# A fused BigBird attention and FNet mixer on one core: another order and split of the last output stores, and in the second batch a mask that moves between TensorE and VectorE by the planner's reckoning

## The chip, the cores and the metric

The kernel runs on one core of one Trainium2 chip. The metric is the device time of one execution in microseconds. The kernel before was timed six times: median 1064.39 us, from 1063.14 to 1068.95. "PE" is TensorE, "DVE" VectorE, "ACT" ScalarE, "POOL" GpSimd, and "SP" SyncE, which issues most of the DMAs.

## The reference

Four batches, eight heads, 768 positions, head width 64, all float32. Attention with a block mask (blocks of 32: neighbours, first and last block, three random blocks per row), then a Fourier mix, a normalization and a two-layer channel product:

```python
scores = np.where(mask, scale * q @ k.T, -1e9)
attn   = exp(scores - max); attn /= attn.sum(-1)          # per head
x      = (attn @ v), heads side by side                    # (4, 768, 512)
u      = x + real(fft(fft(x, axis=1), axis=2))
un     = (u - mean(u)) / sqrt(var(u) + 1e-6)
out    = u + relu(un @ w_ch1) @ w_ch2                      # 512 -> 2048 -> 512
```

## The kernel before

**Order.** Everything is written out in one order by hand-made Python loops (a manual schedule); each engine runs its instructions in that order. The order is chosen while the program is built by a planner: `when["PE"]`, `when["ACT"]`, `when["DVE"]` and `when["POOL"]` are its reckoned clocks, `busy` advances one, `bank` and `give` stand for PSUM banks. What it reckons is a guess with fixed prices; what it puts out is an order.

**Attention.** Two heads make a pair, four pairs a batch (`pairs`, numbered n from 0 to 15). A pair has two halves of 384 queries, and each half has six units, one for each 128 keys, so there are 192 units, numbered u0 to u191; u48 to u95 are the second batch. A slot is two units. For a unit, `scores` (L569) puts the products of two heads into one of two PSUM tiles `s`; `weigh` turns them into weights `e` (one of four SBUF tiles); `values` (L642) multiplies them by v one slot later, and `gather` adds them up over the keys into `acc` for the softmax sums.

The mask is applied in one of two ways. For a unit in `by_pe`, PE adds a product of two small bf16 factors to the scores (L579), and ACT takes the exponent straight into `e` (L589). For the others ACT takes the exponent in place in PSUM (L597), and DVE multiplies by the 0/1 mask and writes `e` (L599). In the first case the `s` tile is free after ACT, in the second after DVE. The line that decides is

```python
if n < NP or masks["by_pe"]:
    by_pe.add(u)
```

where n < NP is the first batch, and `masks["by_pe"]` becomes False in `go`, the step that puts the first batch's channel products into the queue `late`. In this kernel that happens just before u100. `gather` lets DVE add (L623, both heads in one instruction) where the unit is in `by_pe` and the planner's clocks say that DVE is sooner; otherwise POOL adds (L628, one instruction per head).

**The mixer** of batch b runs beside the attention of batch b+1. Its steps before the channel products stand in `apart` and are put in by `gap` wherever the planner sees room: `norm_steps`, the folds (L774 to L802), `along` and `across` (Fourier products), `spread` and `whiten` (normalization, with two small POOL instructions for the root at L913 and L915), `un_flip` (four transposes, tile `utp`, L965, copied by ACT at L966), and `right` (differences for the channel products, L1002). The channel products are fast-multiplication schemes with seven products instead of eight: `quad` (L1040) for the first layer, `channels` (L1096) for the second, and for the last batch `outputs` (L1159).

**x and its stores.** `place` turns a pair's output (transposes `xt`, L665) and ACT copies it into `x` (L666). There are two x tiles for each half of the positions, so batch b reuses the tile of batch b-2 and ACT has to wait until the stores of that tile have landed. `store` (L1107) writes one third (m) of a half; `_rows` gives the row patterns. For half 0, m = 0 and 2, it is two DMAs of 64 rows; for half 1, m = 0 and 2, it is one DMA of 2x64 rows; m = 1 is 1 + 63 + 63 + 1 rows in half 0 and 1 + 2x63 + 1 in half 1. SP issues them in order.

**The last outputs.** `outputs(r, m, after)` runs for r = 0, 1 and m = 0, 1, 2, and r = 1 stores. Each call makes seven products p (PSUM tiles `m` with two buffers, `t` and `o` with one, `s` with two), and DVE adds them into a0, a1 (columns 0:256 and 256:512 of half 0) and b0, b1 (of half 1). `ahead(1)` to `ahead(4)` are the DVE differences that the next m needs. In the kernel before the seven products end in a0, a0, u, b1 and a1, u, a1, b0, and for the last m the stores stand so: b1 after the fifth product, half 0 whole after the sixth, and b0 at the very end, in two pieces of 128 columns, one issued by SP and one by ACT.

After the stores every engine meets `tc.If(over > 0)` (L1574), a branch over a general version that these inputs do not take, and the program ends when all DMAs have landed.

Of the kernel before, what the change touches and what calls it, by code (L numbers as in the profile page):

```python
# [82 lines left out]
def _rows(view, tile):  # L83

    got = []
    for t, p0, runs, jump, n, s0, step in _ORDER:
        if t != tile:
            continue
        at = view[s0:s0 + 1, :]
        row, col = list(at.ap[0])[0], list(at.ap[1])  # L90
        if jump > 0:
            got.append((p0, runs * n, bass.AP(tensor=at.tensor, offset=at.offset,
                                              ap=[[jump * row, runs], [step * row, n], col])))
            continue
        for r in range(runs):
            at = view[s0 + r * jump:s0 + r * jump + 1, :]
            got.append((p0 + r * n, n, bass.AP(tensor=at.tensor, offset=at.offset,
                                               ap=[[step * row, n], col])))
    return got
# [3 lines left out]
def kernel(  # L103
# [14 lines left out]
    nc = tc.nc  # L118

    B, H, S, D = q.shape  # L120
    DM = H * D
    FF = w_ch1.shape[1]
    P = 128
# [14 lines left out]
    NP = H // 2  # L138
# [43 lines left out]
    ps_s = ctx.enter_context(tc.tile_pool(name="ps_s", bufs=2, space=PSUM))  # L182
    ps_o = ctx.enter_context(tc.tile_pool(name="ps_o", bufs=1, space=PSUM))
# [5 lines left out]
    when = {"PE": 0.0, "ACT": 0.0, "DVE": 0.0, "POOL": 0.0}  # L189
    free = {"m": [0.0, 0.0], "t": [0.0]}  # L190

    def busy(engine, us, after=0.0):
        when[engine] = max(when[engine], after) + us
        return when[engine]
# [283 lines left out]
    by_pe, to_gather = set(), deque()  # L478
    masks = {"by_pe": True}
# [68 lines left out]
    UP = 2 * C  # L548
    UNITS = len(pairs) * UP
    SLOT = 2  # L550

    def scores(us):

        n, w = divmod(us[0], UP)
        half = w // C
        qT, kT = turned[n, 0], turned[n, 1]
        queries = slice(half * HS, (half + 1) * HS)
        got = []
        for u in us:
            c = u % C  # L560
            s = ps_s.tile([P, 2, 512], FP32, tag="s", name="s")
            got.append((u, s))
            if n < NP or masks["by_pe"]:
                by_pe.add(u)
            busy("PE", 0.72, max(e_at.get(u - SLOT, 0.0), z_at[u % 2]))
            s_at[u] = when["PE"] + HOP
            for i in range(2):
                rows = slice(D * i, D * i + D)
                nc.tensor.matmul(s[:, i, 0:HS], kT[rows, c * P:(c + 1) * P], qT[rows, queries],  # L569
                                 start=True, stop=u not in by_pe)  # L570
        for u, s in got:
            if u not in by_pe:
                continue
            c = u % C
            busy("PE", 0.25)
            s_at[u] = when["PE"] + HOP
            for i in range(2):
                rows = slice(D * i, D * i + D)
                nc.tensor.matmul(s[:, i, 0:HS], of_k[rows, c * P:(c + 1) * P], off_q[rows, queries],  # L579
                                 start=False, stop=True)  # L580
        return got
# [24 lines left out]
    def gather_to(u):  # L606
        while to_gather and to_gather[0] <= u:
            gather(to_gather.popleft())

    def gather(u):  # L610


        n, w = divmod(u, UP)
        half, c = divmod(w, C)
        if c == 0:
            return
        if c == 1:
            acc_of[n, half] = acc_p.tile([P, 2, HS], FP32, tag="acc", name="acc")
        acc, e = acc_of[n, half], e_of[u]
        start = e_of[u - 1] if c == 1 else acc  # L620
        at = max(e_at[u], acc_at.get((n, half), 0.0))
        if u in by_pe and masks["by_pe"] and w < UP - SLOT and max(when["DVE"], at) + 1.0 < max(when["POOL"], at) + 2.9:
            nc.vector.tensor_tensor(out=acc, in0=start, in1=e, op=ALU.add)  # L623
            acc_at[n, half] = busy("DVE", 1.0, at) + HOP
        else:

            for i in range(2):
                nc.gpsimd.tensor_add(out=acc[:, i, :], in0=start[:, i, :], in1=e[:, i, :])  # L628
            acc_at[n, half] = busy("POOL", 2.9, at) + HOP
        e_free[u] = acc_at[n, half]  # L630
# [320 lines left out]
    def mixer(b, xA, xB):  # L951
# [24 lines left out]
        t, s = {}, {}  # L976
# [127 lines left out]
        def store(half, m, cols=slice(0, DM), queue=nc.sync):  # L1104
            x = (xA, xB)[half]
            for p0, cnt, rows in _rows(out[b][:, cols], T * half + m):
                queue.dma_start(out=rows, in_=x[p0:p0 + cnt, m, cols])  # L1107
            if m == T - 1:
                finished.add((b, half))
# [5 lines left out]
        o_t, o_s = {}, {}  # L1115
        DH = DM // 2

        def block(r, k, n):
            return w2_sb[:, 8 * r + 4 * k:8 * r + 4 * k + 4, n * DH:n * DH + DH]
# [25 lines left out]
        def outputs(r, m, after):  # L1145

            if m == 0:
                output_left(m, 1)
                output_left(m, 2)
            a11, a12, a21, a22 = (hs[g, i][:, :, m * P:(m + 1) * P]  # L1150
                                  for i in range(2) for g in range(2))
            a0, a1 = xA[:, m, 0:DH], xA[:, m, DH:DM]
            b0, b1 = xB[:, m, 0:DH], xB[:, m, DH:DM]
            rights = {j: [o_t[j, 0], o_t[j, 1]] for j in (1, 2, 3, 4)}

            def product(pool, tag, a, c):
                ps = pool.tile([P, 512], FP32, tag=tag, name="yy")[:, 0:DH]
                for k in range(4):
                    nc.tensor.matmul(ps, a[:, k, :],  # L1159
                                     c[k // 2][:, k % 2, :] if isinstance(c, list) else c[:, k, :],  # L1160
                                     start=(k == 0), stop=(k == 3))
                busy("PE", 1.75)
                return ps

            def plus(to, a, c=None):
                tt(out=to, in0=a, in1=to if c is None else c, op=ALU.add)
                busy("DVE", 0.43)

            def ahead(j):
                if after is not None:  # L1170
                    output_left(after, j)

            u = sum_p.tile([P, DH], FP32, tag="oT", name="u")
            p1 = product(ps_m, "m", a11, block(r, 0, 0))
            nc.scalar.copy(out=u, in_=p1)
            plus(a0, p1)
            plus(a0, product(ps_m, "m", a12, block(r, 1, 0)))
            if m == 0:
                output_left(m, 3)
                output_left(m, 4)  # L1180
            plus(u, product(ps_t, "t", a21, rights[2]), u)
            plus(a1, u)
            p5 = product(ps_o, "o", o_s[m, 1], rights[1])
            plus(a1, p5)
            ahead(1)
            plus(u, product(ps_s, "s", o_s[m, 3], rights[3]), u)
            both = xB[:, m, :].rearrange("p (n d) -> p n d", n=2)
            tt(out=both, in0=both,
               in1=u.rearrange("p (o d) -> p o d", o=1).broadcast_to([P, 2, DH]), op=ALU.add)
            busy("DVE", 0.7)  # L1190
            plus(b1, p5)
            ends = r == 1 and after is None
            if ends:
                store(1, m, slice(DH, DM))
            ahead(2)
            p3 = product(ps_m, "m", o_s[m, 4], block(r, 1, 1))
            plus(a1, p3)
            if r == 1:
                store(0, m)
            ahead(3)  # L1200
            ahead(4)
            plus(b0, product(ps_s, "s", a22, rights[4]))
            if ends:
                store(1, m, slice(0, P))
                store(1, m, slice(P, DH), nc.scalar)
            elif r == 1:
                store(1, m)

        fl = [[("tm"[h == 1 and m != 1], lambda h=h, m=m: un_flip(h, m), 0.6, 0.55, 0.0)
               for m in range(T)]  # L1210
# [6 lines left out]
              for m, us in (((0, 2), RIGHT), ((1,), COMBINE))]  # L1217
        le = [("d", lambda i=i: left(0, i), 0.0, 0.0, COMBINE) for i in (1, 3, 4)]
        after = ([fl[0][0], sp[1][0]] + le +
                 [fl[0][2], sp[1][2], wh[1][0], fl[0][1], sp[1][1], wh[1][2],  # L1220
                  fl[1][0], fl[1][2], wh[1][1]] + ri[0] + [fl[1][1]] + ri[1])
        rest = []
        for r in range(2 if last else 0):
            rest += [(lambda p=p: quad(p), 7 * PRODUCT) for p in range(4 * r, 4 * r + 4)]
            rest += [(lambda r=r, m=m: outputs(r, m, m + 1 if m + 1 < T else None), 7 * 1.75)
                     for m in range(T)]
# [123 lines left out]
    def slot(sl):  # L1350
# [21 lines left out]
        if paired and len(due) == 2 and due[0] % SP % T == T - 1:  # L1372
            sum_up()
        got = scores(units) if sl < B * SB else ()
        if paired and len(due) == 2:
            sum_up()
# [236 lines left out]
```

## Time and profile before

| | |
|---|---|
| median of six executions | 1064.39 us |
| the profiled execution: its own time / its span | 1066.16 us / 1064.4 us |
| mean granted TensorE clock | 0.994 |
| PE busy | 1037.8 us, 98% of the span |
| L579 mask product on PE, 200 instructions | 327 ns each, 24.9 us together |
| L597 exponent in PSUM, ACT / L589 exponent to `e`, ACT | 792 / 815 ns |
| L599 mask on DVE | 951 ns (92 times) |
| L623 accumulation on DVE / L628 accumulation on POOL | 1039 ns (17 times) / 1043 ns per head |
| L1166 addition of a product, DVE / L1142 difference, DVE | 423 / 684 ns |

The busy share of PE counts overlapping matmuls once. A wait is read from the timeline: the gap before an instruction stands in brackets with what ended it.

The last stores, from the trace (issue: start of the issuing instruction; landing: last completion event). PE's last matmul ends at 1053.15 us. Where a DMA is 64 or 63 rows, 16 or 9 separate completions are seen; where it is 2x64 or 2x63 rows, two.

| issued, us | by | rows x bytes | landed, us |
|---|---|---|---|
| 1028.12 | SP | 64 x 2048 | 1030.42 |
| 1029.65 | SP | 2x64 x 2048 | 1037.60 |
| 1042.01 | SP | 2x63 x 2048 | 1049.98 |
| 1051.36 | SP | 2x64 x 1024 | 1056.26 |
| 1051.99 | SP | 64 x 2048 | 1057.36 |
| 1052.56 | SP | 64 x 2048 | 1058.55 |
| 1053.63 | SP | 2x64 x 512 | 1061.26 |
| 1053.63 | ACT | 2x64 x 512 | 1062.30 |

The packets of the 2x64 stores with 1024-byte rows run from 1052.53 to 1055.92 us; those of 512-byte rows from SP run from 1057.36 to 1060.90 and from ACT from 1059.28 to 1061.75. SP's first wait for completions ends at 1062.32, and the span ends 2.1 us later.

### The profile page before, as it was taken

What the parts mean: (1) busy time and instruction counts of PE and PEld (TensorE: products, weight loads), DVE (VectorE), ACT (ScalarE), POOL (GpSimd) and SP (SyncE); (2) the same over time, 40 slices, a digit from 0 to 9 for tenths busy, and PEclk for the clock granted to TensorE, in tenths of its full rate; (3) what the DMA queues carried; (4) which work ended last, traced back from release to release, by engine and by line L of the source; (5) the groups of instructions that cost most, each with busy time, mean ns of one, the idle gap of its engine ahead of it and who ended that gap; (6) DMA issues with size and microseconds to landing.
All of it is one profiled execution on the core that took longest, in us unless ns stands there. A gap on an engine that the chain in (4) does not pass through costs nothing.

```text
span 1064.4 us, 12409 instructions
## 1 busy us (share of the span) xinstructions
PE 1037.8 (98%) x4390; PEld 537.1 (50%) x4390; DVE 654.5 (61%) x1218; ACT 374.2 (35%) x742; POOL 235.6 (22%) x262
## 2 busy tenths in 40 slices
PE   8989999999999999999999999999999999999995
PEld 4433445444455554444444555444445554578584
DVE  5888995667645445664668364765457355574663
ACT  6978755664030112343441302353221211210210
POOL 1000073537000001454553001256520001000000
PEclk9999999999999999999999999999999999999998
DMA  7756522220000002212230001221000001000001
GB/s 208 223 178 214 133 46 39 52 47 15 1 0 1 1 0 47 59 29 54 42 55 1 1 0 30 60 38 27 11 11 5 1 0 34 27 0 1 1 20 42
DMA packets 120741, 46.65 MB, mean 44 GB/s; under 512 B 108114, under 2 KB 113632, under 8 KB 120672
## 3 DMA queue, kind: packets, MB, share of 16 engines
q1 hardware_dynamic: 118654, 44.92, 17.1%
q10 hardware_dynamic: 1986, 0.85, 0.3%
q8 instruction: 36, 0.59, 0.2%
q14 instruction: 33, 0.27, 0.1%
q0 software_dynamic: 32, 0.01, 0.0%
HBM read 37.11 MB, written 6.29 MB: 41 GB/s over the span
## 4 chain that ended last, share of the span: by engine, by line
PE 90%; DVE 3%; ACT 2%; DMA 2%; issue 1%; POOL 0%; SPq 0%; ACTq 0%; POOLq 0%; DVEq 0%
PE y L1096 23%; PE z L1040 15%; PE s L569 12%; PE o L642 11%; PE yp L1040 7%; PE yy L1159 7%; PE xp L1040 4%; PE zp L850 2%; PE s L579 1%; DMA out_dram<-x 1%; PE sp L709 1%; PE zp L822 1%; PE sp L723 1%; PE utp L965 1%; PE xt L665 1%
## 5 line engine op out<-in xcount | busy, mean ns | idle before, releaser
L628 POOL TENSOR_TENSOR acc<-acc,e 128x384 f32<-128x384 f32 x158 | 159.3, 1043 | 94.1 <-DVE e L599 75.1
L569 PE MATMUL s<-qT,kT 64*128 64x384 f32 x768 | 153.8, 516 | 8.8 <-ACT e L589 5.3
L642 PE MATMUL o<-e,vr 128*64 128x384 f32 x768 | 142.0, 497 | 0.0
L1096 PE MATMUL y<-w_sb,hB 128*128 128x512 f32 x288 | 128.2, 596 | 1.0 <-DVE x L1099 1.0
L1096 PE MATMUL y<-w_sb,hA 128*128 128x512 f32 x288 | 128.4, 595 | 0.0
L599 DVE TENSOR_TENSOR e<-s,mask 128x768 f32<-128x768 f32 x92 | 83.9, 951 | 57.7 <-ACT s L597 48.0
L1099 DVE TENSOR_TENSOR x<-y,x 128x512 f32<-128x512 f32 x72 | 49.7, 691 | 110.9 <-PE y L1096 110.7
L569 PEld LDWEIGHTS s<-qT,kT 64*128 64x128 f32 x768 | 64.0, 186 | 86.9 <-issue 22.1
L597 ACT ACTIVATE s<-s 128x768 f32<-128x768 f32 x92 | 69.9, 792 | 87.6 <-PE s L569 87.0
L628 POOL TENSOR_TENSOR acc<-e 128x384 f32<-128x384 f32 x42 | 47.1, 1142 | 213.9 <-ACT e L589 128.9
L1040 PE MATMUL z<-unT,t 128*128 128x384 f32 x256 | 93.1, 486 | 1.2 <-DVE hA L1045 1.2
L1045 DVE TENSOR_TENSOR hA<-z,hA 128x384 f32<-128x384 f32 x64 | 35.7, 558 | 87.2 <-PE z L1040 87.2
L589 ACT ACTIVATE e<-s 128x768 f32<-128x768 f32 x100 | 76.1, 815 | 36.9 <-PE s L579 31.8
L1096 PEld LDWEIGHTS y<-w_sb,hB 128*128 128x128 f32 x288 | 53.4, 190 | 67.7 <-issue 64.8
L913 POOL TENSOR_SCALAR st<-st 128x1 f32<-128x1 f32 x24 | 8.6, 358 | 346.9 <-DVE st L912 346.9
L1096 PEld LDWEIGHTS y<-w_sb,hA 128*128 128x128 f32 x288 | 53.3, 190 | 62.8 <-issue 59.7
L642 PEld LDWEIGHTS o<-e,vr 128*64 128x64 f32 x768 | 48.0, 136 | 70.5 <-issue 68.1
L1049 ACT ACTIVATE hA<-hA 128x384 f32<-128x384 f32 x64 | 33.5, 523 | 120.3 <-DVE hA L1045 119.9
L1040 PEld LDWEIGHTS z<-unT,t 128*128 128x128 f32 x256 | 48.5, 190 | 35.5 <-DVE hA L1045 2.1
L1049 ACT ACTIVATE hB<-hB 128x384 f32<-128x384 f32 x64 | 33.5, 523 | 86.5 <-DVE hB L1045 84.2
L1060 ACT COPY hA<-xp 128x384 f32<-128x384 f32 x32 | 15.3, 478 | 97.9 <-PE xp L1040 97.9
L1040 PE MATMUL xp<-unT,w_sb 128*128 128x384 f32 x128 | 47.2, 492 | 0.0
(202 smaller groups left out, 1433.2 us busy)
## 6 DMA issues: line engine op xcount, KB each, us to landing
wraw<-in_moe_w_ch_dram SPq DMA_DIRECT2D x32, 512.0 KB
vr<-in_v_dram SPq DMA_DIRECT2D x30, 192.0 KB
qb<-in_q_dram SPq DMA_DIRECT2D x44, 96.0 KB
kb<-in_k_dram SPq DMA_DIRECT2D x44, 96.0 KB
x<-oT SPq DMA_DIRECT2D x192, 12.0 KB
out_dram<-x SPq DMA_DIRECT2D x17, 128.0 KB
out_dram<-x SPq DMA_DIRECT2D x7, 256.0 KB
qr<-in_q_dram SPq DMA_DIRECT2D x24, 64.0 KB
```

The costliest lines, as they stand in the source:

```text
L569: nc.tensor.matmul(s[:, i, 0:HS], kT[rows, c * P:(c + 1) * P], qT[rows, queries], start=True, stop=u not in by_pe)
L589: nc.scalar.activation(out=e, in_=s[:, :, 0:HS], func=ACT.Exp, scale=scale)
L597: nc.scalar.activation(out=s[:, :, 0:HS], in_=s[:, :, 0:HS], func=ACT.Exp, scale=scale)
L599: nc.vector.tensor_tensor(out=e, in0=s[:, :, 0:HS], in1=m.broadcast_to([P, 2, HS]), op=ALU.mult)
L628: nc.gpsimd.tensor_add(out=acc[:, i, :], in0=start[:, i, :], in1=e[:, i, :])
L642: nc.tensor.matmul(o[D * i:D * i + D, :], vt[:, i, c, :], e[:, i, :], start=(c == 0), stop=(c == C - 1))
L1040: nc.tensor.matmul(to, a[:, k, :], c[:, k, :], start=(k == 0), stop=(k == ND // 2 - 1))
L1045: tt(out=to, in0=ps, in1=a, op=ALU.add)
L1049: nc.scalar.activation(out=h, in_=h, func=ACT.Relu)
L1096: nc.tensor.matmul(y, hs[0, half][:, l, m * P:(m + 1) * P], w2_sb[:, 4 * r + l, :], start=(l == 0), stop=(l == 3))
L1099: nc.vector.tensor_tensor(out=x[:, m, :], in0=y, in1=x[:, m, :], op=ALU.add)
L1159: nc.tensor.matmul(ps, a[:, k, :], c[k // 2][:, k % 2, :] if isinstance(c, list) else c[:, k, :], start=(k == 0), stop=(k == 3))
```

## The change

Three places change.

1. In `scores` a unit of the second batch is masked by PE only where the planner's DVE clock is more than 1 us past its PE clock, and otherwise by DVE.
2. In `outputs` the order of the products becomes a0, a0, u, b0, u, b1 and a1, a1; three of the four `ahead` differences move behind the sixth product's additions.
3. The stores move with them. For the last m the half 0 store is split into columns 0:256 (after the second product) and 256:512 (at the very end), and the half 1 store into columns 0:256 (after the fifth product, from ACT) and 256:512 (after the sixth product, from SP). For m = 0 and 1 the half 1 store now comes before the half 0 store.

```diff
+        behind_pe = when["DVE"] > when["PE"] + 1.0
-            if n < NP or masks["by_pe"]:
+            if n < NP or masks["by_pe"] and behind_pe:
                 by_pe.add(u)
...
+            ends = r == 1 and after is None
             plus(a0, product(ps_m, "m", a12, block(r, 1, 0)))
+            if ends:
+                store(0, m, slice(0, DH))
...
             plus(a1, u)
-            p5 = product(ps_o, "o", o_s[m, 1], rights[1])
-            plus(a1, p5)
-            ahead(1)
+            plus(b0, product(ps_s, "s", a22, rights[4]))
             plus(u, product(ps_s, "s", o_s[m, 3], rights[3]), u)
             both = xB[:, m, :].rearrange("p (n d) -> p n d", n=2)
             tt(out=both, in0=both, in1=u..., op=ALU.add)
+            if ends:
+                store(1, m, slice(0, DH), nc.scalar)
+            p5 = product(ps_o, "o", o_s[m, 1], rights[1])
             plus(b1, p5)
-            ends = r == 1 and after is None
-            if ends:
-                store(1, m, slice(DH, DM))
+            if r == 1:
+                store(1, m, slice(DH if ends else 0, DM))
+            plus(a1, p5)
+            ahead(1)
             ahead(2)
+            ahead(3)
             p3 = product(ps_m, "m", o_s[m, 4], block(r, 1, 1))
             plus(a1, p3)
             if r == 1:
-                store(0, m)
-            ahead(3)
+                store(0, m, slice(DH if ends else 0, DM))
             ahead(4)
-            plus(b0, product(ps_s, "s", a22, rights[4]))
-            if ends:
-                store(1, m, slice(0, P))
-                store(1, m, slice(P, DH), nc.scalar)
-            elif r == 1:
-                store(1, m)
```

In `gather` the condition of the accumulation only gets a name (`sooner`).

Because the planner's clocks depend on the choice, the built program changes in more places than the diff. Put side by side, the two instruction orders differ so on PE:

- u50/51, u68/69, u70/71, u88/89 and u96/97 lose the PE mask, u102/103 get it (before, they were masked by DVE); so 92 units instead of 100 have the PE mask, 16 mask matmuls fewer, and 8 DVE masks more.
- The last `un_flip` of the first batch moves from the slot of u96 to just behind u100/101; `go` comes later, and the first `quad` starts behind u106/107 instead of behind u102/103.
- One set of three small transposes (`st`, L736) moves behind the values of u50/51, and another into that first `quad`.
- One third of the first batch's last `channels` step (half 1, m = 0) and an `un_flip` move from behind u110/111 to before the `xt` transposes and u108/109. Its store now stands ahead of a k load on SP's queue.
- From there on PE's order is the same up to `outputs`. On the other queues, two units' accumulations move from DVE to POOL overall (15 instead of 17 on DVE).

## The prediction

> **What bounds the kernel now.** I read the page's busy shares and its chain first, then the order in which the changed program's instructions stand, then the timeline at each place where the two orders differ.
>
> ```profile
> PE 1037.8 (98%) x4390; PEld 537.1 (50%) x4390; DVE 654.5 (61%) x1218; ACT 374.2 (35%) x742; POOL 235.6 (22%) x262
> ...
> PE 90%; DVE 3%; ACT 2%; DMA 2%; issue 1%; POOL 0%; SPq 0%; ACTq 0%; POOLq 0%; DVEq 0%
> ```
>
> PE is the bound. So a change counts by the PE work it takes away, by the PE gaps it makes or closes, and by the 11 us after PE's last matmul. A masked slot of the second batch, in the timeline:
>
> ```profile
> 202.42 1.56 PE L569 MATMUL s<-qT,kT 64*128 64x384 f32 x8
> 203.82 0.49 PE L579 MATMUL s<-factors 64*128 64x384 bf16 x4
> 204.24 1.51 PE L642 MATMUL o<-e,vr 128*64 128x384 f32 x8
> ```
>
> From the last score matmul to the first of `values` it is 0.74 us here and 0.42 in the slot of u100, which has no PE mask: the PE mask costs 0.32 us a slot. Next, the start of the channel products:
>
> ```profile
> 241.97 1.78 PE L569 MATMUL s<-qT,kT 64*128 64x384 f32 x8 [0.41 <-DVE e L599]
> ...
> 246.14 3.88 DVE L751 TENSOR_TENSOR x<-x,r 128x512 f32<-128x512 f32 x3
> ...
> 250.54 0.59 PE L1040 MATMUL z<-unT,t 128*128 128x384 f32 x1 [1.15 <-DVE hA L1045]
> ```
>
> PE waits 0.41 us at u102 (and 0.11 at u103) because DVE masked u100/101 late, and 1.15 us in the first `quad`, because three L751 stood ahead of the sum it needs. Then two places where ACT stands still for the stores of the x tile that it is to refill:
>
> ```profile
> 411.37 1.11 SPq L1107 DMA_DIRECT2D out_dram<-x  x2
> ...
> 414.65 0.48 ACT L666 COPY x<-xt 128x384 f32<-128x384 f32 x1 [2.98 <-DMA kb<-in_k_dram]
> ...
> 416.88 0.92 PE L569 MATMUL s<-qT,kT 64*128 64x384 f32 x4 [1.28 <-DVE e L599]
> ```
>
> ```profile
> 443.04 0.48 ACT L666 COPY x<-xt 128x384 f32<-128x384 f32 x1 [1.85 <-DMA out_dram<-x]
> ...
> 445.32 0.92 PE L569 MATMUL s<-qT,kT 64*128 64x384 f32 x4 [0.74 <-DVE e L599]
> ```
>
> The exponents of u108 and u112 queue behind those copies, DVE's masks behind the exponents, and PE loses 1.28 and 0.74 us. (The first wait is put down to the k load; the two stores just before it landed at 414.26, and ACT went on then.) Last, the end, from the timeline and SP's waits:
>
> ```profile
> 1051.25 1.89 PE L1159 MATMUL yy<-ot,hB 128*128 128x256 f32 x8
> 1051.36 2.82 SPq L1107 DMA_DIRECT2D out_dram<-x  x4
> 1053.17 0.42 DVE L1166 TENSOR_TENSOR x<-yy,x 128x256 f32<-128x256 f32 x1 [1.30 <-PE yy L1159]
> 1053.63 1.38 ACTq L1107 DMA_DIRECT2D out_dram<-x  x1
> ```
>
> ```profile
> SPq L1574 <- SPq L1574: 8.1, 1, 8.1
> ```
>
> After the last addition SP waits 8.1 us for the stores.
>
> **The masks, slot by slot.** They change only in six slots: five lose the PE mask (-0.32 us each), one gets it (+0.32). What each then waits is worked out from DVE's new order with the table's durations; exponents follow each other at 0.71 us, masks at 0.9, and a restarted PE loses 0.11.
>
> - u50/51: DVE ends its table copies and one sum at 133.05, so its masks end at 133.95 and 134.9. PE, 0.32 + 0.47 earlier (mask gone, transposes moved behind), wants u52 at 133.57 and u53 at 134.3 and gets them at 134.0 and 134.87, where before u53 was at 135.10; the 0.47 of transposes is still to come: +0.24.
> - u68/69 and u70/71: Fourier products stand between these slots and their `values`; the masks end 5 us and more before they are needed. The k flip on DVE goes 2 us later and is needed only at u72. -0.64.
> - u88/89: the order on DVE is mask, accumulation, mask. Second mask done at 215.25 + 0.8 + 0.95 + 1.04 + 0.95 = 219.0; u91 stands at 218.55. Wait 0.45 + 0.11, less 0.32: +0.2. Three accumulations of that half go to POOL, idle then; the normalization roots queue behind them and DVE's L925 waits some 2.5 us for the later one, where PE needs nothing of it for 5 us.
> - u96/97: DVE was idle from 226.9 to 234.2. -0.32.
> - u100 to u103: order on DVE mask, two accumulations, mask. Counted from u100's start the first mask ends at 2.75, the second at 2.75 + 2.08 + 0.95 = 5.8; u103 stands at 1.5 + 0.65 (the moved `un_flip`) + 1.5 + 0.74 = 4.4. Wait 1.4, plus 0.32 for the new PE mask, less the 0.52 waited before: +1.2. This is the worst known: if POOL runs beside the four wide L1002 ahead of it, these take up to 1.48 us as their slowest row does, not 0.68, which is 3.2 more. POOL has one accumulation there (to about 235.3), so two of them at most: I put 0 and keep 1.6 for the range.
> - The first `quad` now stands behind u107, with DVE's L751 after its additions: the 1.15 us goes. Late next would be DVE's masks of u106/107 for the `s` tiles of that `quad`, done 0.9 us before. -1.15. If they are late, this falls to 0.
>
> Sum: 0.24 - 0.64 + 0.2 - 0.32 + 1.2 - 1.15 = -0.5 us.
>
> The Trainium skill, "SBUF — State Buffer", section "SBUF: two separate sides", says that the port pair of VectorE and GpSimd is an exclusive lock held for a whole instruction, which speaks against handing work to either while the other runs. The L751 above show it: 3.88 us for three, alone 0.68 each. With its rule each of the two L1002 would wait for a whole 1.04 us POOL addition, so the sum would be +1.6 instead of -0.5.
>
> **The store waits.** One `channels` third (16 instructions, 3.6 us) and one `un_flip` (0.6) now run before `xt`. Half 0's stores are issued where they were and land 2.9 us after SP's first issue; the copy comes 4.2 us later than it did, at some 415.0 against the 414.3 at which they landed: no wait, -1.28. Half 1's first store goes out some 8 us earlier (at 423.04 before). It takes 8 us (landed 431.04), the next then ran to 437.81 and the third to 442.94, each beginning when the last had landed; the same chain now ends near 437.5, before the copy at 441: -0.74. SP's k load stands behind that store and lands up to 8 us later; DVE flips k only near 447. Bounds: 0 and -2.02; I take -2.0, since both margins (0.7 and 3.5 us) are on the right side.
>
> **The outputs.** The work is the same. The two adders of the `m` bank now stand behind three differences: after the sixth product's end DVE needs 0.2 + 0.46 + 0.34 + 3 x 0.6 + 0.42 = 3.2 us, and the next m's second product, which takes that bank, begins 3.3 us after it. Four such places (two r, m to m+1). I take 0.1 us each, +0.4; bounds 0 and 4 x 0.3 = 1.2 (one weight load and a hop late).
>
> **The end.** The stores of 2x64 rows land with two completions and run at 53 ns per KB row (64 rows in 3.39 us), while 64 rows land with sixteen in 2.3 us. Before, ACT's rows began at 1059.28, as SP's rows thinned out: they share two servers. With T for PE's end, the last m now issues: ACT 2x64 x 1 KB at T - 2.1 (both-addition ended 2.28 before T), SP 2x64 x 1 KB at T - 1.1, SP 64 + 64 rows at T + 0.48. First rows come 1.17 us after issue (1052.53 after 1051.36). The two servers begin at T - 0.95, have 2 x 3.4 + 0.4 us, times 1.15 for idle time as before (9.2 us for some 8.0 of rows): T + 7.3, landed at T + 7.65. Before it was 1062.30 - 1053.15 = T + 9.15. -1.5 us. Bounds: +0.5 (ACT's rows as late as before, 5.65 us after issue, and slower) and -4.5 (two pairs of servers).
>
> The Trainium skill, "DMA: Bandwidth & Descriptors", section "Why a DMA increments its semaphore by 16 and not by 1", has it that a DMA runs on the largest number up to 16 that divides its slowest dimensions, and on the lowest-numbered engines; so two for 2x64, the same for ACT and SP. That speaks against the split by issuer: by it the bytes on these two (128 KB each side by side before and after) are the same, and only the earlier start and the dropped 2 KB rows count, about -1.2. The rows above agree.
>
> **Sum.** -0.5 - 2.0 + 0.4 - 1.5 = -3.6 us. Against the profiled execution 1066.16 - 3.6 = 1062.6 (span 1060.8); that execution lies 1.77 above the median, so the median is predicted at 1064.39 - 3.6 = **1060.8 us**, -0.34%. Within 0.3% (3.2 us) I call it the same: this is about what a measurement of this kernel can tell from no change.
>
> **Rivals.**
> 1. *Slower: VectorE is the late one.* At u50, u88, u96 and u100 its masks end two accumulations (2.1 us) later than needed, and the unmasked slots u104 to u107 wait 0.53 each as u102/103 did. Against my 0.55 + 0.56 + 0 + 1.4 that is 5.9 more, and 1.06, and the 1.15 of the first `quad` stays: +8.1, so 1068.9. It speaks for it that POOL and DVE slow each other; against it, DVE's 7 idle us before u96. It ends slower once these waits exceed my count by 6.8 us.
> 2. *The store waits stay* (another landing, such as that of the moved store, holds ACT): 1062.8, the same.
> 3. *The end gives nothing*: the same bytes on the same two servers, or ACT's rows late: 1062.3, the same.
> 4. *The change does less than it says*: 44 of the second batch's units keep the PE mask, and the orders are mere reshuffling: 0 within 0.5 us of 1064.4. The closed 2.0 us speaks against it.
> 5. *All as counted, and the end has two pairs of servers*: 1060.8 - 3 = 1057.8.
>
> **How the numbers follow.** As counted, within -5 to -3.2 us: 0.43, and case 5: 0.09, so faster 0.52. Same: as counted but short of 3.2 us 0.12, case 2 0.10, case 3 0.10, case 4 0.04: 0.36. Slower, case 1: 0.12. The range goes from 1058.2 (case 5 nearly) to 1066.0, which leaves out case 1's full price; the likeliest case alone is 1059.4 to 1062.5.
>
> **What would show it.** In the profile after: 184 mask matmuls at L579, 100 masks at L599 and 15 at L623; no gap near 250 and none at u110 and u114; gaps of about 0.5 at u52 and u91 and 1.4 at u103; `outputs` no longer than 12.3 us each; SP's last wait near 6.5 us instead of 8.1 and the span's end about 9.7 us after PE's last matmul instead of 11.2. I am wrong if a new wait for the x tile appears, if u103 waits over 3 us, or if ACT's store lands as late after PE's end as before.

## The result, and the profile after

The changed kernel takes 1062.21 us (median; 1061.38 to 1064.94) where the kernel before takes 1064.47 in the same comparisons: ratio 0.9978, 95% interval 0.9972 to 0.9984, so -2.3 us. The forecast was 1060.8, with a range of 1058.2 to 1066.0. The sign is certain, and the size lies within the 0.3% that the prediction called the same. It gave that 0.36, and 0.52 to a gain of more than 0.3%, so the outcome is not the one it held likeliest.

The changed kernel's profiled execution took 1063.4 us with a span of 1061.7; clock 0.997. Its busy shares and the chain that ended last:

```profile
PE 1037.1 (98%) x4374; PEld 535.3 (50%) x4374; DVE 660.7 (62%) x1224; ACT 374.6 (35%) x742; POOL 236.6 (22%) x266
...
PE 89%; DVE 4%; ACT 2%; issue 1%; POOL 1%; DMA 1%; SPq 0%; ACTq 0%; POOLq 0%; DVEq 0%
```

PE lost the 16 mask matmuls, 0.7 us of busy time, and is still the bound. In the code after, scores are at L570, the PE mask at L580, the DVE mask at L600, accumulations at L625 (DVE) and L630 (POOL), `values` at L644, the sums product `sp` at L725, the `x` copy at L668, `quad` at L1042, stores at L1109 and the branch at L1577.

To see where the 2.3 us come from, I compare starts of the same PE work in both traces, counted from the start of u40. The start of a program varies from one execution to the next (u28, for one, moves by over 1 us between executions whose code is the same up to there), but from u40 on two traces of the same code agree to 0.03 us in nearly all these stretches and to 0.08 in the worst (u100 to u118, before and "new outputs only"; 0.10 in all up to `outputs`).

| stretch, us | before | after | difference | forecast |
|---|---|---|---|---|
| u40 to u64 (u50/51) | 50.11 | 51.43 | +1.32 | +0.24 |
| u64 to u72 (u68 to u71) | 24.48 | 23.83 | -0.65 | -0.64 |
| u72 to u92 (u88/89) | 40.41 | 40.88 | +0.47 | +0.2 |
| u92 to u100 (u96/97; `un_flip`, 0.65, moves out) | 17.16 | 16.34 | -0.82 | -0.32 - 0.65 |
| u100 to the second `quad` (the same `un_flip` in) | 22.09 | 22.60 | +0.51 | +1.2 - 1.15 + 0.65 |
| second `quad` to u118 (stores of batch 0) | 191.04 | 190.05 | -0.99 | -2.0 |
| u118 to the first of `outputs` | 492.27 | 492.33 | +0.06 | 0 |
| first of `outputs` to PE's last end | 109.19 | 109.38 | +0.19 | +0.4 |
| PE's last end to the span's end | 11.22 | 8.99 | -2.23 | -1.5 |
| sum | | | -2.14 | -3.6 |

So before PE's last stretch nothing is gained (-0.10 us up to `outputs`, no more than two traces of the same code differ by), and the end gives all of it. First the places that the prediction named. DVE's mask, two accumulations and the next mask ahead of u103, and PE's wait for it, in the timeline:

```profile
240.48 0.96 DVE L600 TENSOR_TENSOR e<-s,mask 128x768 f32<-128x768 f32 x1 [1.40 <-POOL acc L630]
241.35 1.94 DVE L625 TENSOR_TENSOR acc<-acc,e 128x768 f32<-128x768 f32 x2
...
243.21 0.95 DVE L600 TENSOR_TENSOR e<-s,mask 128x768 f32<-128x768 f32 x1
...
244.22 0.92 PE L570 MATMUL s<-qT,kT 64*128 64x384 f32 x4 [1.44 <-DVE e L600]
```

That is the 1.4 us of the forecast. The wait at u91 is there too, 0.51 against 0.45, and the fifth product of the first `quad` waits for nothing:

```profile
219.39 0.92 PE L570 MATMUL s<-qT,kT 64*128 64x384 f32 x4 [0.51 <-DVE e L600]
```

```profile
256.74 1.45 PE L1042 MATMUL z<-unT,t 128*128 128x384 f32 x4
```

Then the stretch of the stores. The copy into x has no bracket (nor has the next one, at 441.54), and PE has none before u110 and u114, so the 1.28 and 0.74 us are gone. But PE has three new brackets:

```profile
411.59 3.70 PE L1098 MATMUL y<-w_sb,hB 128*128 128x512 f32 x8 [0.35 <-DVE x L1101]
...
416.25 0.49 ACT L668 COPY x<-xt 128x384 f32<-128x384 f32 x1
```

```profile
430.05 0.66 PE L967 MATMUL utp<-ident,un 128*128 128x128 f32 x4 [0.24 <-DVE sums L693]
...
433.77 1.56 PE L1042 MATMUL z<-t,w_sb 128*128 128x384 f32 x4 [0.48 <-DVE t L1004]
```

And the end: ACT's store and SP's three, from the timeline, and what SP waits for after its last issue (total, times, longest):

```profile
1050.47 1.13 ACTq L1109 DMA_DIRECT2D out_dram<-x  x1
...
1051.46 2.91 SPq L1109 DMA_DIRECT2D out_dram<-x  x3
1052.74 0.43 DVE L1168 TENSOR_TENSOR x<-yy,x 128x256 f32<-128x256 f32 x1 [0.97 <-PE yy L1161]
```

```profile
SPq L1577 <- SPq L1577: 5.4, 3, 4.6
```

Where SP waited 8.1 us in one piece before, it waits 5.4 in three: the last three stores land one after the other, at 1059.09, 1059.49 and 1059.82. PE's last matmul ends at 1052.70, so the last landing is 7.12 us after it; before it was 9.16.

### The profile page after: what moved, and what is told of

Read it like the earlier page. It is cut to its first block, busy times and chain, and to the rows that moved or that the text cites. A ratio compares the mean times of both kernels' runs of the same rounds, so it can differ in the third digit from the quotient of the medians.

```text
span 1061.7 us, 12394 instructions
## 1 busy us (share of the span) xinstructions
PE 1037.1 (98%) x4374; PEld 535.3 (50%) x4374; DVE 660.7 (62%) x1224; ACT 374.6 (35%) x742; POOL 236.6 (22%) x266
## 4 chain that ended last, share of the span: by engine, by line
PE 89%; DVE 4%; ACT 2%; issue 1%; POOL 1%; DMA 1%; SPq 0%; ACTq 0%; POOLq 0%; DVEq 0%
PE y L1098 23%; PE z L1042 16%; PE s L570 11%; PE o L644 10%; PE yp L1042 8%; PE yy L1161 7%; PE xp L1042 4%; PE zp L852 2%; PE sp L711 1%; PE zp L824 1%; PE s L580 1%; POOL acc L630 1%; PE utp L967 1%; DVE t L1004 1%; PE xt L667 1%
## 5 line engine op out<-in xcount | busy, mean ns | idle before, releaser
L630 POOL TENSOR_TENSOR acc<-acc,e 128x384 f32<-128x384 f32 x162 | 164.2, 1049 | 91.5 <-DVE e L600 73.3
L570 PE MATMUL s<-qT,kT 64*128 64x384 f32 x768 | 154.5, 518 | 8.8 <-ACT e L590 5.7
L644 PE MATMUL o<-e,vr 128*64 128x384 f32 x768 | 141.7, 497 | 0.0
L600 DVE TENSOR_TENSOR e<-s,mask 128x768 f32<-128x768 f32 x100 | 91.2, 951 | 63.9 <-ACT s L598 52.7
L570 PEld LDWEIGHTS s<-qT,kT 64*128 64x128 f32 x768 | 64.4, 187 | 86.8 <-issue 24.3
L598 ACT ACTIVATE s<-s 128x768 f32<-128x768 f32 x100 | 75.8, 792 | 91.6 <-PE s L570 89.3
L630 POOL TENSOR_TENSOR acc<-e 128x384 f32<-128x384 f32 x42 | 45.5, 1105 | 215.1 <-ACT e L590 128.8
L1042 PE MATMUL z<-unT,t 128*128 128x384 f32 x256 | 93.1, 486 | 0.0
L644 PEld LDWEIGHTS o<-e,vr 128*64 128x64 f32 x768 | 47.9, 136 | 69.9 <-issue 66.8
L590 ACT ACTIVATE e<-s 128x768 f32<-128x768 f32 x92 | 70.0, 814 | 36.0 <-PE s L580 25.5
L1042 PEld LDWEIGHTS z<-unT,t 128*128 128x128 f32 x256 | 48.6, 190 | 34.1 <-DVE hA L1047 0.4
L1042 PE MATMUL z<-t,w_sb 128*128 128x384 f32 x128 | 46.7, 488 | 1.0 <-DVE t L1004 1.0
```

Source lines behind the costliest of these rows:

```text
L590: nc.scalar.activation(out=e, in_=s[:, :, 0:HS], func=ACT.Exp, scale=scale)
L598: nc.scalar.activation(out=s[:, :, 0:HS], in_=s[:, :, 0:HS], func=ACT.Exp, scale=scale)
L600: nc.vector.tensor_tensor(out=e, in0=s[:, :, 0:HS], in1=m.broadcast_to([P, 2, HS]), op=ALU.mult)
L644: nc.tensor.matmul(o[D * i:D * i + D, :], vt[:, i, c, :], e[:, i, :], start=(c == 0), stop=(c == C - 1))
L1042: nc.tensor.matmul(to, a[:, k, :], c[:, k, :], start=(k == 0), stop=(k == ND // 2 - 1))
```

## The experiments

All ratios are to the kernel before, measured beside it (its median there was 1064.38 to 1064.88 us), so runs are compared by their ratios. The last columns are from each profile; "to `outputs`" is from u40 to the first product of `outputs`, "landing" (of the last store) and "end" (of the span) are counted from PE's last matmul. The two runs with rows spread write some rows of the output in each other's place; they measure, and are no kernels to keep.

| run | median, us | ratio, interval | to `outputs` | landing | end |
|---|---|---|---|---|---|
| before | 1064.47 | 1 | 837.56 | 9.16 | 11.22 |
| after | 1062.21 | 0.9978, 0.9972 to 0.9984 | 837.46 | 7.12 | 8.99 |
| new outputs only | 1062.56 | 0.9981, 0.9972 to 0.9990 | 837.66 | 6.99 | 9.05 |
| new masks only | 1064.65 | 0.9999, 0.9990 to 1.0008 | 837.43 | 9.22 | 11.26 |
| last rows spread | 1060.43 | 0.9958, 0.9943 to 0.9974 | 837.44 | 3.75 | 7.18 |
| no ACT store | 1060.94 | 0.9964, 0.9951 to 0.9977 | 837.45 | 5.83 | 7.69 |
| u50/51 alone | 1063.65 | 0.9995, 0.9985 to 1.0004 | 838.93 | 6.94 | 8.81 |
| clean masks | 1059.92 | 0.9959, 0.9945 to 0.9972 | 835.65 | 6.86 | 8.73 |
| early rows spread | 1063.22 | 0.9992, 0.9983 to 1.0001 | 836.44 | 9.26 | 11.21 |
| half 1 first | 1060.01 | 0.9960, 0.9944 to 0.9975 | 837.43 | 4.52 | 6.70 |
| both | 1058.14 | 0.9942, 0.9925 to 0.9959 | 835.59 | 4.43 | 6.36 |
| last sums on DVE | 1062.39 | 0.9977, 0.9967 to 0.9987 | 837.19 | 7.14 | 9.01 |
| both, more on PE | 1057.88 | 0.9939, 0.9922 to 0.9955 | 835.39 | 4.52 | 6.54 |
| all | 1062.01 | 0.9970, 0.9956 to 0.9985 | 839.25 | 4.44 | 6.38 |

### The two halves of the change

Outputs and stores of the changed kernel, masks of the kernel before:

```diff
-            if n < NP or masks["by_pe"] and behind_pe:
+            if n < NP or masks["by_pe"]:
```

> The new outputs and stores, with the masks of the kernel before. Theory (nearly all of the measured 2.3 us comes from the end; masks and store waits cancel): the end after PE's last matmul is 9.0 us instead of 11.2, the outputs cost 0.2, so -2.0 us against the kernel before, about 1062.4, and the waits of 1.28 and 0.74 us at u110 and u114 are there again. Rival, the forecast as it stood (end -1.5, outputs +0.4): -1.1 us, 1063.3. Second rival (masks and stores carry the gain): 0.

The other way round, the kernel before with the mask rule alone:

```diff
+        behind_pe = when["DVE"] > when["PE"] + 1.0
-            if n < NP or masks["by_pe"]:
+            if n < NP or masks["by_pe"] and behind_pe:
```

> The new mask rule, with outputs and stores of the kernel before. Theory: the masks cost about 0.9 us up to the second quad, the moved store step gives 0.9 back, so 0 within 0.4 us of the kernel before; no wait at u110 and u114, but waits of 0.5 at u91, 1.4 at u103, about 0.4 before u59, and PE about 1 us later at u64 than a plain count of the mask matmuls says. Rival, the forecast as it stood: -0.5 and -2.0, so -2.5 us, 1062.0.

The outputs alone give 0.9981 (-2.0 us), the masks alone 0.9999: the two add up to the whole. With the outputs alone the two store waits are back:

```profile
415.33 1.78 PE L570 MATMUL s<-qT,kT 64*128 64x384 f32 x8 [1.32 <-DVE e L600]
...
443.81 0.59 PE L570 MATMUL s<-qT,kT 64*128 64x384 f32 x2 [0.76 <-DVE e L600]
```

So the masks and the store waits do cancel: +0.83 us up to the second `quad`, -0.93 behind it. The forecast's -2.5 for these two terms is excluded: it would be a ratio of 0.9977, and the interval begins at 0.9990.

### Why u50/51 costs 1.3 us instead of 0.24

Only these two masks moved, with the outputs of the changed kernel:

```diff
-            if n < NP or masks["by_pe"] and behind_pe:
+            if n < NP or masks["by_pe"] and u not in (50, 51):
```

> The changed kernel's outputs, and of the masks only u50/51 moved to DVE. Theory (those two masks push DVE's folds and POOL's accumulations of that half into each other, so that pair 4's sums reach PE late): gaps of 0.4 before u59 and 0.3 inside the sums, PE 1.1 us later at u64 than with the old masks, and the whole 1.1 us slower than the run with the outputs alone, which stood at ratio 0.9981: about 0.9991. Rival, the forecast as it stood (+0.24 here): ratio 0.9983. Second rival (the loss comes from u68 to u71 or later): nothing lost before u64.

0.9995, where the outputs alone had 0.9981: +1.5 us. The two intervals overlap, so the traces decide: +1.27 up to `outputs`, and all of it is there at u64. The lines that show it, first of the kernel with the outputs alone, then of this one, POOL's four accumulations for u58/59 and PE's sums product of pair 4; this one's begin with PE's wait at u59:

```profile
147.91 6.16 POOL L630 TENSOR_TENSOR acc<-acc,e 128x384 f32<-128x384 f32 x4 [2.63 <-DVE acc L625]
...
153.54 1.42 PE L725 MATMUL sp<-acc,pick 128*32 128x384 f32 x8
```

```profile
144.79 0.92 PE L570 MATMUL s<-qT,kT 64*128 64x384 f32 x4 [0.42 <-ACT e L590]
...
147.84 7.72 POOL L630 TENSOR_TENSOR acc<-acc,e 128x384 f32<-128x384 f32 x4 [5.43 <-DVE acc L625]
...
153.91 1.41 PE L725 MATMUL sp<-acc,pick 128*32 128x384 f32 x6
155.62 0.83 PE L725 MATMUL sp<-acc,pick 128*32 128x384 f32 x2 [0.30 <-POOL acc L630]
```

The same four POOL instructions begin at the same time and take 1.56 us longer. In the first kernel one of DVE's two widest folds (1536 elements, L776) runs beside them, in the second both, because masks and accumulations that DVE took on stand ahead of the folds. One by one the four take 2.38, 1.71, 1.00 and 1.18 us in the first kernel and 2.39, 2.52, 1.77 and 1.17 in this one, so what is added is one more instruction beside a wide fold. The folds here:

```profile
147.61 1.75 DVE L776 TENSOR_TENSOR sa<-x 128x1536 f32<-128x1536 f32 x1
149.28 2.56 DVE L776 TENSOR_TENSOR sd<-x 128x1536 f32<-128x1536 f32 x1
```

PE, which came 0.33 us earlier to u52 and is still 0.23 ahead at u58, loses 0.39 at u59, where ACT's exponent (and before it a DVE accumulation) is late. It loses 1.12 in the sums product, which needs the last accumulation: from 153.91 to 156.45 it takes 2.54 us instead of 1.42. The first form also explains why the old kernel's trace did not warn: eight `sp` products take 0.85 us when nothing is late (below), and there they took 1.42 with no bracket, since a wait inside a row of joined instructions shows none.

To test that POOL is the cause, its work was taken away: DVE adds u58 and u59 up ahead of its folds.

```diff
-        if u in by_pe and masks["by_pe"] and w < UP - SLOT and sooner:
+        if u in by_pe and masks["by_pe"] and (w < UP - SLOT and sooner or u in (58, 59)):
```

> The run with only u50/51 moved to DVE (ratio 0.9995), but the accumulations of u58 and u59 are done by DVE ahead of its folds instead of by POOL beside them. Theory (the four POOL instructions of u58/59, slowed from 6.2 to 7.7 us by DVE's folds, make the sums of pair 4 late for PE): the 0.3 us gap in the sums and the 1.1 us at u64 go, unless the folds, some 2 us later, are late for the Fourier products: -1.1 us, ratio 0.9985. Rival (PE is late at u64 for another reason, such as the order of its own transposes): the 1.1 us stays, 0.9995.

```profile
150.68 0.85 PE L725 MATMUL sp<-acc,pick 128*32 128x384 f32 x8
```

0.9977, 1.9 us better than with u50/51 alone (1.74 up to `outputs` by the traces); u40 to u64 falls from 51.40 to 50.21, and another 0.48 us goes before u72. More than the expected 1.1 comes back, since PE can now do the sums product one slot earlier, in 0.85 us instead of 2.54. So POOL's lateness is the cause of the 1.12 us. The wait at u59 stays (0.40 here); it is not POOL's. That the folds are what slows POOL is read from the overlap in the traces; no run changed the folds alone.

### The masks that cost no wait, and the next wait

```diff
-            if n < NP or masks["by_pe"] and behind_pe:
+            if n < NP or masks["by_pe"] and u not in (68, 69, 70, 71, 96, 97):
```

> The changed kernel's outputs, and DVE takes the masks of u68 to u71 and u96/97 only, where the changed kernel showed no wait; u50/51, u88/89, u100/101 and u102/103 are masked by PE, and the first quad stands behind u107. Theory: 3 x 0.32 less for the masks, 1.15 less for the first quad's gap, 0.5 less wait but 0.64 more mask at u100 to u103, and 0.9 less in the stretch of the stores: -2.5 us against the run with the outputs alone (ratio 0.9981), so about 0.9957. Rival (PE's gain here only meets the next wait, as at u64): less than 1 us, so 0.9972 or more.

0.9959, so -2.3 us against the outputs alone; -2.01 of it up to `outputs`. u70 and u72 come 0.33 and 0.32 us earlier, as counted. But with no wait left at u103, the next one stands at u106, where DVE's masks stand behind differences (L1004) of 1.10 to 1.24 us each:

```profile
246.60 1.78 PE L570 MATMUL s<-qT,kT 64*128 64x384 f32 x8 [1.42 <-DVE e L600]
```

### The stores of batch 0

The kernel before, with half 1's early stores as DMAs of 64 rows. To have a positive row step the rows of each 64 are written in reversed order.

```diff
-        if jump > 0:
+        if jump > 0 and joined:
...
-            at = view[s0 + r * jump:s0 + r * jump + 1, :]
+            first = s0 + r * jump + min(step, 0) * (n - 1)
+            at = view[first:first + 1, :]
...
-                                               ap=[[step * row, n], col])))
+                                               ap=[[abs(step) * row, n], col])))
...
-            for p0, cnt, rows in _rows(out[b][:, cols], T * half + m):
+            for p0, cnt, rows in _rows(out[b][:, cols], T * half + m, last):
```

> The kernel before, but in batches 0 to 2 the half 1 stores of m = 0 and 2 go as two DMAs of 64 rows each instead of one of 2x64 rows. For a positive row step the rows of each 64 are written in reversed order, so these thirds of the output have rows exchanged; the bytes are the same. Theory (ACT's copies at u112 wait for the 8 us that a 2x64 store takes): half 1's stores land within some 3 us of their issue, the 0.74 us gap at u114 goes, the 1.28 at u110 (half 0's stores) stays: -0.7 us, ratio 0.9993. Rival (the wait is for something else): both gaps stay, 0.

```profile
414.90 1.78 PE L570 MATMUL s<-qT,kT 64*128 64x384 f32 x8 [1.30 <-DVE e L600]
...
442.54 1.56 PE L570 MATMUL s<-qT,kT 64*128 64x384 f32 x8
```

The first half 1 store, 8.0 us as one DMA (423.04 to 431.04), now lands 2.9 us after its first issue (421.07 to 423.95), with 16 completions each instead of two. The wait at u114 goes, the one at u110 (half 0's stores) stays: ratio 0.9992, whose interval includes 1; in the trace 1.12 us less up to `outputs`, of which 0.8 at u114 and the rest by u117. The 0.74 us was indeed the price of the narrow DMA.

### The end

Three runs change only the last third. First the same rewriting of rows for the changed kernel's last half 1 stores (`joined` is `not (last and m == T - 1)`), so that 64-row DMAs take the place of 2x64:

> The changed kernel, but the last third's half 1 stores (m = 2) go as 64 rows each instead of 2x64 rows, so two DMAs where there was one. To have a positive row step, the rows of each 64 are written in reversed order, so this third of the output has its rows exchanged; the bytes are the same. Theory (two servers bound the end): the last landing is set by the last 64-row store, issued 1.0 us after PE's last matmul and landing 2.3 later, at +3.3 instead of +7.1: -3.5 us against the changed kernel (-3.0 to -3.8), about 1058.7. Rival (the end is a fixed time for any last store, or bound by bytes): within 0.5 us of the changed kernel.

Then ACT's store issued by SP:

```diff
-                store(1, m, slice(0, DH), nc.scalar)
+                store(1, m, slice(0, DH))
```

> The changed kernel, but the half 1 store of columns 0:256 of the last third is issued by SP instead of ACT, at the same place in the order. Theory (ACT's and SP's rows run in sequence on the same two servers): the last landing moves by less than 0.4 us, the time by -0.4 to +0.4 against the changed kernel. Rival (ACT's queue has a share of its own): the second 2x64 store begins only when the first has landed, and the end is 1 to 3 us later.

Then, on top of that, half 1 completed earlier:

```diff
-            plus(a0, product(ps_m, "m", a12, block(r, 1, 0)))
-            if ends:
-                store(0, m, slice(0, DH))
+            if not ends:
+                plus(a0, product(ps_m, "m", a12, block(r, 1, 0)))
...
             plus(a1, p5)
+            if ends:
+                plus(a0, product(ps_m, "m", a12, block(r, 1, 0)))
+                store(0, m, slice(0, DH))
```

> The changed kernel with all stores issued by SP, and for the last third the product that completes half 0's columns 0:256 comes after the fifth product instead of second, so that half 1's two 2x64 stores are issued about 1.9 us earlier against PE's end, and half 0's first store later. Theory (the two servers no longer bound the end; SP, which takes its branch 2.3 us after PE's last matmul and needs 2.9 us to come out of it, does): the last landing is near +4.0 us after PE's last matmul instead of +5.8, but SP's first wait can't end before +5.2, so -0.5 us against the same kernel without this move (ratio 0.9964): 0.9959. Rival (the last landing alone sets the end): -1.8 us, 0.9947.

What SP waits for after its last issue, in the kernel with the rows spread, then without an ACT store, then with half 1 first:

```profile
SPq L1578 <- SPq L1578: 2.9, 1, 2.9
```

```profile
SPq L1577 <- SPq L1577: 3.5, 3, 3.2
```

```profile
SPq L1579 <- SPq L1579: 2.9, 1, 2.9
```

- Spread rows land 3.75 us after PE's end instead of 7.12: the two servers (what carries the rows of a 2x64 store, two side by side, as its two completions show) do bound the changed kernel's end. But the time falls by some 2 us only, where 3.5 was expected. SP takes its branch at 1054.75 and shows its first instruction behind it at 1057.69, 1.39 us after the last landing (1056.30). This 2.9 us is a second bound that I had not counted here.
- Without the ACT store the ratio is 0.9964 for 0.9978, 1.5 us less, and the last landing comes 1.29 us earlier (+5.83 for +7.12), outside the 0.4 that I expected, and on the side that neither theory had. The two completions of each 2x64 store tell where: 1055.50 and 1056.02, then 1058.21 and 1059.09 in the changed kernel; 1054.66 and 1054.69, then 1057.38 and 1057.40 here. One of the two servers lost up to 0.9 us. In the changed kernel ACT takes the branch at 1051.63, behind its store, and comes out at 1057.06; without that store it takes it at 1041.56 and is out at 1047.41, before the last stores. The likely cause is code fetched for ACT by a packet or two of the instruction queues (8 KB, 0.31 to 0.44 us each; six of them begin between 1053.7 and 1059.0 in the changed kernel, three between 1053.3 and 1056.0 here) on that server; the trace does not say which server a packet used, so this is argued, not shown.
- With half 1 first, the last landing is at +4.52, and SP's first wait behind its branch ends 0.03 us after it (taken at 1053.48, first wait at 1056.39): the two bounds meet, and this run does not tell which of them held. The span's end moves 0.99 us, between the 0.5 and the 1.8 of the two theories. The ratios, 0.9960 for 0.9964, are too close to tell the two kernels apart, so the step is shown by the traces alone; the branch came earlier than I had put it, 1.65 us after PE's end instead of 2.3, because the last issue took 0.59 us instead of 1.20.

### Faster kernels

Clean masks and half 1 first together; then u104 to u107 on PE as well; then u58/59 added up by DVE as well:

```diff
-            if n < NP or masks["by_pe"] and behind_pe:
+            if n < NP or masks["by_pe"] and u not in (68, 69, 70, 71, 96, 97) or 104 <= u < 108:
```

(the first run without the last condition; the third with the accumulation edit shown above).

> The masks of the run with the clean slots alone (ratio 0.9959) and the end of the run with half 1 first (0.9960, against 0.9978 for the changed kernel). Theory (the two are independent): 0.9959 - 0.0018 = 0.9941, -6.3 us. Rival (one of the two gains was the other's): 0.9955 or more.

> The first kernel of this set with u104 to u107 masked by PE too, which removes the masks for which PE waited 1.42 us before u106. Theory: 2 x 0.32 more mask, 1.5 less wait: -0.9 us, so 0.9933 where that one is 0.9941. Rival (another wait takes the place of this one, such as the first quad's): 0 to +0.6 us against it.

> The kernel with half 1 first, the clean masks and u104 to u107 on PE (ratio 0.9939), with the accumulations of u58 and u59 on DVE as well, which with the u50/51 masks gave 1.9 us back, of which by the score times 0.6 us is more than the loss it was to undo. Theory (the old kernel too waits for POOL at pair 4's sums): -0.6 us, ratio 0.9934. Rival (that gain belongs to the moved masks alone): 0.9939.

The first gives 0.9942: the two gains add up. The second, 0.9939, can't be told from it: the 1.42 us at u106 go, but masks of 0.64 come, and the first `quad` waits again; the column of the starts says 0.20 us in all.

```profile
256.68 1.56 PE L1042 MATMUL z<-unT,t 128*128 128x384 f32 x4 [0.32 <-DVE hA L1047]
```

The third loses, 0.9970; by the traces it is 3.86 us longer up to `outputs` than the second. With u50/51 on PE one wide fold runs ahead of the accumulations, and the copy of the sums product (L693) stands on DVE behind four more steps of the folds (L780, L787 to L789), where with the last sums on DVE it stood ahead of them. PE's transposes `xt` wait 2.58 us for that copy, and the scores behind them (u64/65) take 2.83 instead of 1.56:

```profile
157.18 0.90 PE L667 MATMUL xt<-ident,oT 128*128 128x128 f32 x3 [2.58 <-DVE sums L693]
```

So the edit that repaired one order harms another. Two versions thus take 6.2 to 6.5 us off the kernel before, about 4 more than the change.

## Why the prediction was right or wrong

The total was 1.4 us too low. Two steps fell short by 2.15 us together, and the end gave 0.73 more than counted, so that the errors partly cancel. That the time still fell is due to the end alone: of the 2.5 us that masks and store waits were to give, the traces show 0.10.

- **u50/51, +0.24: wrong, +1.32.** This is the step that failed. DVE's masks were followed only to u52/53; I did not follow the folds that they push back, nor who shares that time with them. What was followed was misread, too: the set of transposes `st` ahead of u52 stays there (133.88 before, 133.03 after), and the one that moves stood behind the scores of u52/53 already. So the wait of 0.43 at u52 did not come (PE lost 0.11 there), PE was 0.20 us ahead at u58 instead of 0.24 behind, and what was not followed cost 1.52: 0.39 at u59 and 1.13 in the sums. The prediction had the price (L751 slowed beside POOL, 3.88 us for three), but looked for it at u100, where the last wide L1002 (L1004 now) ran at 0.65 and 0.68 us, undisturbed. The lock rule of the Trainium skill ("SBUF — State Buffer", section "SBUF: two separate sides"), which the prediction weighed and left out, put the masks at +1.6, because of u100; they came to +0.83, by such a slowdown, but at u58. There POOL and DVE do take turns: POOL's first addition begins during a fold and ends 0.86 us after it (149.37 to 150.23 with u50/51 alone), and the fold that begins during that addition takes 2.56 us instead of 1.75.
- **The store waits, -2.0: half wrong, -0.93.** The mechanism was right: both waits closed, since no copy waits for a landing any more. But in the same stretch PE now has the three waits of 0.35, 0.24 and 0.48 us shown above. The kernel before has all three a batch later, where no such store wait stands ahead of them (which suggests that the store waits hid them; no run took them away):

```profile
661.95 2.41 PE L1096 MATMUL y<-w_sb,hB 128*128 128x512 f32 x5 [0.35 <-DVE x L1099]
...
680.41 0.66 PE L965 MATMUL utp<-ident,un 128*128 128x128 f32 x4 [0.24 <-DVE sums L691]
...
684.12 1.56 PE L1040 MATMUL z<-t,w_sb 128*128 128x384 f32 x4 [0.47 <-DVE t L1002]
```

- **u68 to u71, u96/97, u100 to u103 and the first `quad`: right, within 0.2.** -0.65 for -0.64; -0.17 for -0.32 (the stretch less the 0.65 of the `un_flip`); -0.14 for +0.05; the wait of 1.44 at u103 was forecast as 1.4. **u88/89**: +0.47 for +0.2; the gap itself was right (0.51 for 0.45), the rest is small losses without a bracket.
- **The outputs, +0.4: right in sign, +0.19**, nearer the lower bound of 0.
- **The end, -1.5: mechanism right, size short, -2.23.** ACT's rows begin 0.94 us before PE's end (0.95 forecast) and SP's begin when they thin out, as said: one pair of servers. The oversized term is the 15% of idle time between rows, 1.1 us: the rows run from 1051.76 to 1058.97, 7.2 us for the 7.2 that were counted without it. Against that, the last landing came 0.85 us after them, where 0.35 was counted. No run separates the earlier start of these rows from the dropped 2 KB rows. The Trainium skill's rule ("DMA: Bandwidth & Descriptors", section "Why a DMA increments its semaphore by 16 and not by 1") agrees with the pair, as the run with the last rows spread shows (16 completions a store for two, and a landing 3.4 us earlier); the -1.2 worked out with it was further off.
- **Rival 1 (slower: VectorE is late)** did not come: its masks were as late as counted (0.51 at u91, 1.44 at u103) or less (u52). POOL and DVE did slow each other, as it said, but that cost PE 1.1 us at the sums, where it had 8.1 in all. **Rival 5 (two pairs of servers)** is excluded by the order of the rows. **Rival 2**, with 0 for the store stretch, was as near to -0.93 as the -2.0, but not for its reason: no landing held ACT. **Rival 3**'s 1062.3 is the number nearest to the result, by luck: the end, which it put at nothing, gave all.

## What to carry to other kernels

When an engine off the critical path is given work, follow what it pushes back until someone waits, and ask of each moved instruction which other engine it will now run beside; here two masks of 0.94 us cost PE more at a sums product some 20 us later than they saved. A closed wait is worth its length less the waits that the neighbouring, undisturbed stretches of the same loop show; read these off a later batch first. At the end of a program, count for every engine not only the landing but when it takes its last branch, and try letting engines that are done take theirs before the last stores: it went with 1.29 us here, in one pair of runs and with the cause not shown.

## What was not expected of the hardware

- SP came out of its last branch 2.9 us after taking it where every store had landed 1.4 us before (last rows spread; 2.6 in "both"), and the span can't end before it: spreading the rows brought the landing 3.4 us forward and the span's end only 1.8 us (8.99 to 7.18 after PE's end).
- An ACT store shortly before the end made the last landing 1.29 us later than the same store from SP.
- POOL's four accumulations took 7.72 us beside two wide DVE folds and 6.16 beside one. A fold that began while POOL was adding took 2.56 us (with u50/51 alone) and 2.13 (an earlier one, outputs only); one that began just before POOL, or with POOL idle (last sums on DVE), took 1.75.
